# First chunk of an adaLN transformer block: row tile 1 normalised on ScalarE, scale columns in two steps, another PSUM bank order

## The chip, the cores and the metric

The kernel runs on one core of one Trainium2 chip. The metric is device time in microseconds (us), and lower is better. Engines are named as the profile names them: PE is TensorE's matmuls, PEld its weight loads, DVE is VectorE, ACT is ScalarE, POOL is GpSimd, SP is SyncE, which here issues every transfer. "q1" below is the first weight load of the q projection, and "Exp" the first Exp of the first chunk.

Ratios are the mean time of one kernel's fast runs over that of the other's in the same rounds, so they are not quite the ratio of the medians quoted.

## The reference, cut to what matters

```python
mod = (silu(c) @ w_mod)            # six rows of 1024: sa, ca, ga, sb, cb, gb
h   = layernorm(x) * (1 + ca) + sa # x is 2048 x 1024, bf16
qkv = h @ wqkv                     # 1024 -> 3 x 1024; q and k go through phi(t) = t>0 ? t+1 : exp(t)
...                                # linear attention, output projection, then x + ga * (...)
h   = layernorm(x) * (1 + cb) + sb
x   = x + gb * ((silu(h @ w_gate) * (h @ w_up)) @ w_down)   # F = 3584
```

Here ca is the scale and sa the shift of the first layernorm. The kernel computes both as columns (features on partitions) with tiny matmuls: WCA and WSA are the slices of w_mod that they need, 2 MB each, loaded in two halves.

## The kernel before

A helper records every operation, derives the semaphores, and emits one program per engine in the recorded order. The row axis is worked in four chunks of 512 rows (four row tiles of 128). Apart from the bank order, which also sets the PSUM banks of the next 40 groups of q and k matmuls, the change touches only the first chunk, in roughly the first 28 us. (A group is the eight accumulating matmuls that fill one PSUM bank.)

The loads stand in this order in SP's queue. None of them waits for any compute:

```python
for st in range(4): P.dma("x0_%d" % st, XRES[:, st, :], xv[:, st, :])   # 4 row tiles of x
ca_load(0)                 # scale columns 0-3, 1 MB
wq_load(0, 2)              # q weights, k-tiles 0 and 1
ca_load(1)                 # scale columns 4-7
wq_load(2, 2)
sa_load(1)                 # shift columns 4-7: the "first WSA half"
wq_load(4); wq_load(5); wq_load(6); wq_load(7)
sa_load(0)                 # shift columns 0-3: the "second WSA half"
# ... x of the second chunk, k weights, more x ...
```

Statistics, normalisation and transposes of the first four row tiles; `warm(n)` issues n dummy matmuls on zeros, meant to keep PE's clock up:

```python
act_stats(2)                                   # statistics of tile 2 on ACT
warm(13, bank=3)
s0_[0](); s0_[1](); s1_[0](); s0_[2](); ln1_rstd1(0); s1_[1]()   # DVE; the power -1/2 is on POOL
ln1_xn(0); tile_transposes(0); warm(2, bank=3)
s1_[2](); ln1_rstd1(1); s3_[0]()
ln1_xn(1); tile_transposes(1); warm(4, bank=3) # tile 1 normalised on DVE
# ... statistics of tiles 2 and 3 ...
ln1_xn(2); ln1_xn(3)
mod_sc(WCA, 8, range(4)); fin_ca(0, 4)         # scale columns 0-3: 32 matmuls, then one DVE op
tile_transposes(2, 3)                          # k-tile by k-tile, both tiles
h0_first(0..3, "dve")                          # k-tiles 0-3: transposed x * scale, PSUM to SBUF
raw_copy(4); raw_copy(6)                       # k-tiles 4-7 unscaled, on ACT
```

The q projection of the chunk accumulates 8 k-tiles. K-tiles 0 to 3 enter without the shift, which a bias adds later. K-tiles 4 to 7 need scale and shift, so they need the first WSA half:

```python
# k-tiles 0 and 1 of the first seven q groups (14 matmuls)
mod_sc(WCA, 8, range(4, 8)); fin_ca(4, 4)
for nt in range(7):
    if nt == 6:
        mod_sc(WSA, 0, range(4, 6))   # <- gate 1: needs the first WSA half
        fin_sa(4, 2); h0_scale(4); h0_scale(5)
    q_part(nt, qb[nt], (2, 3))
mod_sc(WSA, 0, range(6, 8)); fin_sa(6, 2); h0_scale(6); h0_scale(7)
# k-tiles 4, 5, 6 of seven groups (21 matmuls)
for nt in range(7):
    if nt == 0:
        mod_sc(WSA, 0, range(4))      # <- gate 2: needs the second WSA half
        fin_sa(0, 4, True)
    if nt == 4:
        bias_mm()                     # the shift of k-tiles 0-3, as a bias for q
    q_part(nt, qb[nt], (7,))
# eighth group, then Exp and Relu of every q group with that bias
```

Of the kernel before, what the change touches and what calls it, by code (L numbers as in the profile page):

```python
# [8 lines left out]
ACT = mybir.ActivationFunctionType  # L9
# [255 lines left out]
def bass_adaLN_cond__linear_attn_block__swiglu_ffn__prompt_kernel(  # L265
# [22 lines left out]
    with ExitStack() as es:  # L288
# [6 lines left out]
        def T(name, off, shape, dt):  # L295
            n = 1
            for s_ in shape[1:]:
                n *= s_
            assert off % 32 == 0 and off + n * mybir.dt.size(dt) <= ARENA, (name, off, shape)
            return nc.alloc_sbuf_tensor_at(name, shape, dt, offset=base + off)  # L300
# [4 lines left out]
        WCA = T("wca", 32 * KB, [128, NDT, D], BF16)  # L305
# [35 lines left out]
        HT = T("ht", 120 * KB, [128, 2, NDT, 512], BF16)  # L341
# [52 lines left out]
        P = _Prog()  # L394
# [59 lines left out]
        def warm(n=1, bank=2):  # L454
            for _ in range(n):
                P.pe("matmul", out=PS[:, bank, :], lhsT=IDENT[:], rhs=E1[:, 0, :], start=True, stop=True)
# [6 lines left out]
        def ln1_stats_ops(st):  # L463
            par, j = (st // 4) % 2, st % 4
            return [
                lambda: P.dve("bn_stats", out=STATS[:, par, j, 0, :], in_=XRES[:, st, 0:512]),
                lambda: P.dve("bn_stats", out=STATS[:, par, j, 1, :], in_=XRES[:, st, 512:1024]),
                lambda: P.dve("bn_aggr", out=MV[:, st, :], in_=STATS[:, par, j, :, :]),
            ]
# [10 lines left out]
        def ln1_xn(st):  # L480
            P.dve("tensor_scalar", out=XRES[:, st, :], in0=XRES[:, st, :],
                  scalar1=MV[:, st, 0:1], scalar2=RSTD[:, st:st + 1], op0=ALU.subtract, op1=ALU.mult)
# [7 lines left out]
        def th_dma(st):  # L490
            buf, j = (st // 4) % 2, st % 4
            xbar(HT[:, buf, :, j * 128:(j + 1) * 128], XRES[:, st, :])
# [12 lines left out]
        def mod_sc(w, c0, ms):  # L505
            for m in ms:
                for kt in range(NDT):
                    P.pe("matmul", out=PS[:, 0, c0 + m:c0 + m + 1], lhsT=w[:, kt, m * 128:(m + 1) * 128],
                         rhs=SILUC[:, kt:kt + 1], start=mod_first[0], stop=(kt == NDT - 1), skip_group_check=True)
                    mod_first[0] = False  # L510

        def fin_ca(m, n):
            P.dve("tensor_scalar", out=MODCOL[:, 0, m:m + n], in0=PS[:, 0, 8 + m:8 + m + n], scalar1=1.0, scalar2=None,
                  op0=ALU.add)

        def fin_sa(m, n, cast=False):
            if cast:
                P.dve("tensor_copy", out=MODTMP[:, m:m + n], in_=PS[:, 0, m:m + n])
            P.dve("tensor_copy", out=MODCOL[:, 1, m:m + n], in_=PS[:, 0, m:m + n])
# [12 lines left out]
        def t_view(dt, n=1):  # L532
            return PSB[:, 4 + dt // 2, (dt % 2) * 512:(dt % 2 + n) * 512]

        def h0_first(dt, eng):
            if eng == "act":
                P.act("activation", out=HT[:, 0, dt, :], in_=t_view(dt), func=ACT.Copy, scale=MODCOL[:, 0, dt:dt + 1])
            else:
                P.dve("tensor_scalar", out=HT[:, 0, dt, :], in0=t_view(dt), scalar1=MODCOL[:, 0, dt:dt + 1],
                      scalar2=None, op0=ALU.mult)  # L540

        def raw_copy(dt):
            P.act("activation", out=HT[:, 1, dt:dt + 2, :], in_=t_view(dt, 2).rearrange("p (d q) -> p d q", q=512),
                  func=ACT.Copy)

        def h0_scale(dt):
            P.dve("tensor_scalar", out=HT[:, 0, dt, :], in0=HT[:, 1, dt, :], scalar1=MODCOL[:, 0, dt:dt + 1],
                  scalar2=MODCOL[:, 1, dt:dt + 1], op0=ALU.mult, op1=ALU.add)

        def ln1_rstd1(st):  # L550
            P.dve("tensor_scalar", out=VE[:, st:st + 1], in0=MV[:, st, 1:2], scalar1=EPS, scalar2=None, op0=ALU.add)
            P.pool("tensor_tensor", out=RSTD[:, st:st + 1], in0=VE[:, st:st + 1], in1=NEGHALF[:, 0:1], op=ALU.pow)

        def ln1_xn_act(st):
            P.dve("tensor_scalar", out=NMR[:, st:st + 1], in0=MV[:, st, 0:1], scalar1=RSTD[:, st:st + 1],
                  scalar2=-1.0, op0=ALU.mult, op1=ALU.mult)
            P.act("activation", out=XRES[:, st, :], in_=XRES[:, st, :],
                  func=ACT.Identity, scale=RSTD[:, st:st + 1], bias=NMR[:, st:st + 1])
# [30 lines left out]
        s0_, s1_, s3_ = ln1_stats_ops(0), ln1_stats_ops(1), ln1_stats_ops(3)  # L589
        m2 = act_mv_ops(2)  # L590

        def tile_transposes(*js):
            for dt in range(NDT):
                for j in js:
                    c = (dt % 2) * 512 + j * 128
                    P.pe("transpose", out=PSB[:, 4 + dt // 2, c:c + 128], in_=XRES[:, j, dt * 128:(dt + 1) * 128],
                         identity=IDENT[:])
# [5 lines left out]
        s0_[2]()  # L603
        ln1_rstd1(0)
        s1_[1]()
        ln1_xn(0)
        tile_transposes(0)
        warm(2, bank=3)
        s1_[2]()
        ln1_rstd1(1)  # L610
        s3_[0]()
        ln1_xn(1)
        tile_transposes(1)
        warm(4, bank=3)
        m2[1]()
        m2[0]()
        neg_rstd(2)
# [2 lines left out]
        ln1_rstd1(3)  # L620
        ln1_xn(2)
        ln1_xn(3)
        mod_sc(WCA, 8, range(4))
        fin_ca(0, 4)
        tile_transposes(2, 3)
        warm(0, bank=3)
        h0_first(0, "dve")
        h0_first(1, "dve")
        h0_first(2, "dve")
        h0_first(3, "dve")  # L630
        raw_copy(4)
        raw_copy(6)
        P.act("activation", out=ACTWARM[:], in_=SILUC[:], func=ACT.Exp)

        phi_ctr = [0]
# [32 lines left out]
        def q_part(nt, bank, dts):  # L668
            for dt in dts:
                P.pe("matmul", out=PS[:, bank, :], lhsT=WQK[:, dt, nt * 128:(nt + 1) * 128],  # L670
                     rhs=HT[:, 0, dt, :], start=(dt == 0), stop=(dt == 7))
# [3 lines left out]
        def next_bank():  # L675
            i = qk_ctr[0]
            qk_ctr[0] += 1
            return (i + 1) % 8 if i < 40 else i % 5 + 1

        def q_group(ch, nt):  # L680
            buf, bank = ch % 2, next_bank()
# [45 lines left out]
            P.dma("mdr%d" % i, dst[:], MDR[i].unsqueeze(0).to_broadcast([128, D]))  # L727

        def q_phase_chunk0(side):
            qb = [1, 2, 3, 4, 6, 5, 7]  # L730
            for nts, dts in ((range(6), (0,)), (range(2), (1,)), ((6,), (0, 1)), (range(2, 6), (1,))):
                for nt in nts:
                    q_part(nt, qb[nt], dts)
            mod_sc(WCA, 8, range(4, 8))
            fin_ca(4, 4)
            for nt in range(7):
                if nt == 6:
                    mod_sc(WSA, 0, range(4, 6))
                    fin_sa(4, 2)
                    for dt in (4, 5):  # L740
                        h0_scale(dt)
                q_part(nt, qb[nt], (2, 3))
            mod_sc(WSA, 0, range(6, 8))
            fin_sa(6, 2)
            for dt in (6, 7):
                h0_scale(dt)
            act_stats(4)
            for dt in (4, 5, 6):
                for nt in range(7):
                    q_part(nt, qb[nt], (dt,))  # L750
            for nt in range(7):
                if nt == 0:
                    mod_sc(WSA, 0, range(4))
                    fin_sa(0, 4, True)
                    for f in ln_ops[1]:
                        f()
                    ln1_rstd1(5)
                if nt == 4:
                    bias_mm()
                q_part(nt, qb[nt], (7,))  # L760
            for f in act_mv_ops(4):
                f()
            neg_rstd(4)
            ln1_xn(5)
            ln1_xn(4)
            th_dma(5)
            th_dma(4)
            q_phi = lambda nt: phi_evac(qb[nt] if nt < 7 else 0, PQT[:, nt, 0:512], bias=BIASQ[:, nt:nt + 1])
            for i, dt in enumerate(range(NDT)):
                P.pe("matmul", out=PS[:, 0, :], lhsT=WQK[:, dt, 896:1024], rhs=HT[:, 0, dt, :], start=(i == 0),  # L770
                     stop=(i == 7))
            for dt in range(4):
                h0_shift(dt)
            for nt in range(8):
                q_phi(nt)
                for f in side.get(nt, []):
                    f()
            qk_ctr[0] = 0
# [93 lines left out]

        P.dma("wo", WO[:], wov)
        G_BANKS = [0] + [next_bank() for _ in range(4)]

        MB = next_bank()
# [197 lines left out]
        for ch in range(NCH):  # L1074
            nxt = ch + 1 if ch + 1 < NCH else None
            for ft in range(NFT):
                q = 14 * ch + ft // 2
# [13 lines left out]
                if ch == 0 and ft % 2 == 0 and ft < 14:  # L1091
                    i = ft // 2
# [11 lines left out]
            for j in range(4):  # L1104
# [8 lines left out]
                for nh in range(2):  # L1113
                    i = nh
# [52 lines left out]
```

## Time and profile before

| | before |
|---|---|
| first measurement | 835.99 us, 835.11 to 836.0, 3 runs |
| span of the profiled run | 832.9 us, granted clock 1.0 |

From the page of the kernel before: the busy line, and the chain that ended last, by engine.

```profile
PE 821.7 (99%) x4053; PEld 379.3 (46%) x4132; DVE 301.0 (36%) x657; ACT 195.8 (24%) x335; POOL 43.2 (5%) x56
...
PE 96%; DMA 1%; DVE 1%; SPq 1%; issue 1%; ACT 0%; DVEq 0%
```

Nearly all of the change lies in the first 3% of the span. The chain of the same kernel in order of time, cut to the lines around the first WSA half (columns: start, length, what), says something else about that stage:

```profile
7.95 11.88 DMA wsa<-in_w_mod_dram
19.82 0.05 issue
19.87 3.23 PE ps L178 x42
...
```

From 7.95 to 19.82 us the end of the program hangs on the transfer of the first WSA half, not on a compute engine (before that, on SP issuing loads). The stretch table of the kernel before (columns: stretch, length, busy us of PE, PEld, DVE, ACT, POOL, granted clock, DMA share, GB/s) shows: the 16 DMA engines are full (a share of about 1).

```profile
13.00:20.00 7.00, 6.46 (x61) 3.20 (x64) 1.18 (x4) 3.15 (x4) 0.00 (x0) 1.00 1.08 368
20.00:26.00 6.00, 5.95 (x64) 3.20 (x64) 1.76 (x6) 0.00 (x0) 0.00 (x0) 1.00 1.08 360
...
29.00:45.00 16.00, 15.95 (x75) 7.24 (x74) 15.20 (x49) 15.33 (x28) 1.68 (x3) 1.00 1.03 253
```

The timeline of weight loads before (columns: start, length, engine, operation, shapes, count; in brackets the idle time before it and what ended it) shows the places. They are q1 at 12.96, gate 1 at 19.86 after 0.78 us of waiting, and gate 2 at 25.59 us:

```profile
12.96 0.56 PEld L178 LDWEIGHTS ps<-ht,wqk 128*128 128x128 bf16 x4 [0.22 <-issue]
13.80 0.10 PEld L178 LDWEIGHTS ps<-ht,wqk 128*128 128x128 bf16 x1 [0.28 <-ACT ht L178]
14.07 0.33 PEld L178 LDWEIGHTS ps<-ht,wqk 128*128 128x128 bf16 x3 [0.18 <-DVE ht L178]
14.71 0.98 PEld L178 LDWEIGHTS ps<-ht,wqk 128*128 128x128 bf16 x6 [0.31 <-ACT ht L178]
...
16.81 2.28 PEld L178 LDWEIGHTS ps<-ht,wqk 128*128 128x128 bf16 x12
19.86 0.47 PEld L178 LDWEIGHTS ps<-siluc,wsa 128*128 128x128 bf16 x16 [0.78 <-DMA wsa<-in_w_mod_dram]
...
25.59 1.01 PEld L178 LDWEIGHTS ps<-siluc,wsa 128*128 128x128 bf16 x32 [0.17 <-DMA wsa<-in_w_mod_dram]
```

Weight loads run ahead of the matmuls that use them, so their waits are longer than PE's. At gate 1 PE's matmuls themselves stood idle 0.29 us, by their modelled ends:

```profile
19.87 0.55 PE L178 MATMUL ps<-siluc,wsa 128*128 128x1 bf16 x16 [0.29 <-DMA wsa<-in_w_mod_dram]
```

And the first Exp of ACT in the timeline before, the end of the stage:

```profile
28.86 0.69 ACT L178 ACTIVATE e<-ps,biasq 128x512 bf16<-128x512 f32 x1 [0.29 <-DVE mv L178]
```

### The profile page before, as it was taken

Reading aid. Unit: us, or ns where it says so; the run is one execution under the profiler, and the core shown is the slowest. Engines: PE = TensorE matmul, PEld = TensorE weight load, DVE = VectorE, ACT = ScalarE, POOL = GpSimd, SP = SyncE. Lnnn points to the kernel's source line nnn. Section 1 sums busy time; section 2 is a strip of 40 time slices with the busy share of each in tenths; the row PEclk is TensorE's granted clock in tenths of the full one; section 3 lists DMA queues with packets and bytes.
Section 4 is the critical chain, followed back from the end, with each engine's and each line's share of the span. In section 5 each row is a group of like instructions: output and inputs, shape, how many; then the busy total and the mean of one; then the engine's idle time right before and its main releaser. Section 6 shows DMA issues by size and latency. Waiting matters only on the chain.

```text
span 832.9 us, 10029 instructions
## 1 busy us (share of the span) xinstructions
PE 821.7 (99%) x4053; PEld 379.3 (46%) x4132; DVE 301.0 (36%) x657; ACT 195.8 (24%) x335; POOL 43.2 (5%) x56
## 2 busy tenths in 40 slices
PE   7999999999999999999999999999999999999998
PEld 4544444444444444444444444444444444444444
DVE  5797985657873212110222111122111212111111
ACT  3667642222332111110111111111111111111011
POOL 1000000000050000030000003000000300000000
DMA  9969734938197895610455571045557104553000
GB/s 311 300 151 227 208 70 146 200 103 303 35 223 241 257 268 152 179 50 13 114 152 152 151 189 39 13 114 153 153 152 194 32 13 121 153 150 94 1 26 25
DMA packets 190940, 117.17 MB, mean 141 GB/s; under 512 B 49576, under 2 KB 174640, under 8 KB 190896
## 3 DMA queue, kind: packets, MB, share of 16 engines
q1 hardware_dynamic: 190896, 116.55, 50.7%
q8 instruction: 32, 0.52, 0.3%
q14 instruction: 12, 0.10, 0.0%
HBM read 100.67 MB, written 4.33 MB: 126 GB/s over the span
## 4 chain that ended last, share of the span: by engine, by line
PE 96%; DMA 1%; DVE 1%; SPq 1%; issue 1%; ACT 0%; DVEq 0%
PE ps L178 96%; DMA wsa<-in_w_mod_dram 1%; SPq L178 1%; DVE acc L178 0%; DVE xres L178 0%; DVE mhl L178 0%; ACT mw L178 0%; DVE ve L178 0%; DVE ut L178 0%; DVE mean L178 0%; DVE msq L178 0%; DVE sumx L178 0%; DVEq L249 0%
## 5 line engine op out<-in xcount | busy, mean ns | idle before, releaser
L178 PE MATMUL ps<-h2t,guu 128*128 128x512 bf16 x878 | 210.2, 379 | 0.9
L178 PE MATMUL ps<-h2t,gug 128*128 128x512 bf16 x878 | 210.0, 380 | 0.9
L178 DVE TENSOR_TENSOR at<-sg,ps 128x512 bf16<-128x512 bf16 x112 | 77.1, 688 | 296.1 <-PE ps L178 285.0
L178 ACT ACTIVATE sg<-ps 128x512 bf16<-128x512 f32 x112 | 66.9, 597 | 310.3 <-PE ps L178 298.9
L178 PEld LDWEIGHTS ps<-h2t,guu 128*128 128x128 bf16 x896 | 87.6, 98 | 105.8
L178 PEld LDWEIGHTS ps<-h2t,gug 128*128 128x128 bf16 x896 | 87.4, 98 | 105.4
L178 PE MATMUL ps<-wd_a,at 128*128 128x512 bf16 (+2 forms) x519 | 112.9, 373 | 0.5
L178 PE MATMUL ps<-ht,wqk 128*128 128x512 bf16 x499 | 110.7, 380 | 0.9 <-DVE ht L178 0.3
L178 PE MATMUL ps<-wd_b,at 128*128 128x512 bf16 (+2 forms) x388 | 85.5, 373 | 0.5
L178 PEld LDWEIGHTS ps<-wd_a,at 128*128 128x128 bf16 x528 | 51.0, 98 | 59.8
L178 PEld LDWEIGHTS ps<-ht,wqk 128*128 128x128 bf16 x512 | 49.2, 98 | 59.2 <-ACT ht L178 0.6
L178 DVE TENSOR_TENSOR ut<-att,gb_b 128x512 bf16<-128x512 bf16 (+1 forms) x32 | 13.7, 427 | 167.6 <-ACT att L178 167.6
L178 ACT ACTIVATE att<-ps 128x512 bf16<-128x512 f32 (+1 forms) x32 | 17.4, 591 | 182.1 <-PE ps L178 182.1
L178 PEld LDWEIGHTS ps<-wd_b,at 128*128 128x128 bf16 x396 | 38.2, 98 | 44.7
L178 PE MATMUL ps<-pk,xres 128*128 128x512 bf16 x250 | 56.4, 380 | 0.3
L178 PE MATMUL ps<-mw,pqt 128*128 128x512 bf16 x250 | 55.8, 380 | 0.4
L178 POOL TENSOR_SCALAR h2t<-h2t,modcol 128x512 bf16<-128x512 bf16 x32 | 28.5, 905 | 395.5 <-DMA h2t<-xn 379.2
L178 ACT ACTIVATE e<-ps 128x512 bf16<-128x512 f32 x56 | 33.0, 602 | 32.8 <-PE ps L178 24.7
L178 PEld LDWEIGHTS ps<-mw,pqt 128*128 128x128 bf16 x256 | 24.9, 98 | 29.7 <-DVE xres L178 0.2
L178 PEld LDWEIGHTS ps<-pk,xres 128*128 128x128 bf16 x256 | 24.7, 98 | 29.8 <-issue 0.4
L178 ACT ACTIVATE junk<-xres 128x1024 bf16<-128x1024 bf16 x24 | 25.4, 1058 | 36.0 <-DVE xres L178 35.8
L178 POOL TENSOR_TENSOR rstd<-ve,neghalf 128x1 f32<-128x1 f32 (+2 forms) x17 | 14.0, 838 | 215.7 <-DVE ve L178 176.8
(98 smaller groups left out, 341.4 us busy)
## 6 DMA issues: line engine op xcount, KB each, us to landing
gug<-in_B_w_gate_dram SPq DMA_DIRECT2D x56, 512.0 KB, 4.0
guu<-in_B_w_up_dram SPq DMA_DIRECT2D x56, 512.0 KB, 5.3
xres<-in_A_x_dram SPq DMA_DIRECT2D x20, 256.0 KB, 7.8
rb<-recip_den SPq DMA_DIRECT2D x8, 512.0 KB, 12.0
stgx<-in_w_mod_dram SPq DMA_DIRECT2D x2, 2048.0 KB, 8.6
wd_a<-in_B_w_down_dram SPq DMA_DIRECT2D x4, 1024.0 KB, 7.4
out_dram<-xres SPq DMA_DIRECT2D x31, 128.0 KB, 1.7
xres<-in_A_x_dram SPq DMA_DIRECT2D x3, 1024.0 KB, 14.2
```

What stands on the lines that cost most here:

```text
L178: return getattr(e, method)(**kw)
```

## The change

The intent is to bring the q projection's first matmul forward. Row tile 1 moves to ACT, so that DVE is free sooner for tiles 2 and 3. Only the scale columns that are needed first are made first. One of the two raw copies moves to DVE. The bank order follows the order in which the transpose banks come free. (The joint transposes of tiles 2 and 3, k-tile by k-tile, are in both versions.)

```diff
-        def raw_copy(dt):
-            P.act("activation", out=HT[:, 1, dt:dt + 2, :], in_=t_view(dt, 2).rearrange(...), func=ACT.Copy)
+        def raw_copy(dt, eng):
+            dst, src = HT[:, 1, dt:dt + 2, :], t_view(dt, 2).rearrange("p (d q) -> p d q", q=512)
+            if eng == "act": P.act("activation", out=dst, in_=src, func=ACT.Copy)   # lines joined here
+            else:            P.dve("tensor_copy", out=dst, in_=src)
@@ statistics and normalisation
+        s1_[2]()
+        ln1_rstd1(1)
         ln1_xn(0)
         tile_transposes(0)
-        warm(2, bank=3)
-        s1_[2]()
-        ln1_rstd1(1)
+        warm(5, bank=3)
         s3_[0]()
-        ln1_xn(1)
+        ln1_xn_act(1)          # one DVE op for the bias, then one 1024-column pass on ACT
         tile_transposes(1)
-        warm(4, bank=3)
+        warm(1, bank=3)
@@ scale columns and copies
-        mod_sc(WCA, 8, range(4))
-        fin_ca(0, 4)
+        mod_sc(WCA, 8, range(2))
+        fin_ca(0, 2)
         tile_transposes(2, 3)
-        warm(0, bank=3)
         h0_first(0, "dve")
         h0_first(1, "dve")
-        h0_first(2, "dve")
-        h0_first(3, "dve")
-        raw_copy(4)
-        raw_copy(6)
+        raw_copy(4, "dve")
+        raw_copy(6, "act")
@@ next_bank
-            return (i + 1) % 8 if i < 40 else i % 5 + 1
+            return (1, 2, 3, 4, 6, 7, 5, 0)[i % 8] if i < 40 else i % 5 + 1
@@ q_phase_chunk0
-            qb = [1, 2, 3, 4, 6, 5, 7]
-            for nts, dts in ((range(6), (0,)), (range(2), (1,)), ((6,), (0, 1)), (range(2, 6), (1,))):
+            qb = [1, 2, 3, 4, 6, 7, 5]
+            for nt in range(4):
+                q_part(nt, qb[nt], (0,))
+            mod_sc(WCA, 8, range(2, 4))
+            fin_ca(2, 2)
+            for dt in (2, 3):
+                h0_first(dt, "dve")
+            for nts, dts in (((4, 5), (0,)), (range(6), (1,)), ((6,), (0, 1))):
```

More of the change, by code (lines that the diff above doesn't have):

```diff
@@ L540, in h0_first @@
                       scalar2=None, op0=ALU.mult)
-        def raw_copy(dt):
-            P.act("activation", out=HT[:, 1, dt:dt + 2, :], in_=t_view(dt, 2).rearrange("p (d q) -> p d q", q=512),
-                  func=ACT.Copy)
+        def raw_copy(dt, eng):
+            dst, src = HT[:, 1, dt:dt + 2, :], t_view(dt, 2).rearrange("p (d q) -> p d q", q=512)
+            if eng == "act":
+                P.act("activation", out=dst, in_=src, func=ACT.Copy)
+            else:
+                P.dve("tensor_copy", out=dst, in_=src)
         def h0_scale(dt):
```

## The prediction

> What bounds the kernel. The page shows PE busy 99% of 832.9 us, and the chain that ended last is 96% PE. The change touches only the first 28 us. There the chain in order of time is not PE: until 7.95 us it is SP issuing loads, then 11.88 us of waiting for the first half of WSA (shift columns, landing at 19.83 us), then PE, without a gap over 0.1 us. The stretch table shows the DMA engines full (share 1.06 to 1.09, 350 to 380 GB/s) from 7 to 28 us. The waits show a second gate: PE's weight loads idle 0.17 us for the other WSA half, landing at 25.59 us. From there to 45 us PE is busy 19.3 of 19.4 us. So before 19.83 us PE has slack: its weight loads sat 0.78 us, its matmuls 0.29 us idle there.
>
> What the change does, costed from the trace:
> - Row tile 1's normalisation leaves DVE (0.55 us) for ScalarE: one 1024-column pass (1.06 us for such a pass) plus a 0.15 us DVE op for the bias. ScalarE is free only at 8.27 us, so the pass ends near 9.5 us, where DVE's ended at 9.05. Its transposes come 0.4 us later, in time that dummy matmuls filled before.
> - DVE's chain for tiles 2 and 3 starts earlier: I put the last normalisation's end at 11.2 us instead of 11.85, so the first q matmul comes at 12.6 instead of 13.2 us.
> - Half of the first scale-column matmuls (16 of 32, about 0.4 us) move between the q matmuls. That is later PE work, and eats most of those 0.6 us.
> - One raw copy goes from ScalarE (1.02 us) to DVE: estimated 0.8 us, from 0.48 us for 512 columns there; the Trainium skill ("VectorE: DVE Perf Modes", the perf-mode tier table) caps copies out of PSUM at the 2x mode, and the 0.48 us fits that. It removes PE's waits for ScalarE (0.3 us twice) at 13.8 and 14.7 us.
> - The bank order makes later groups use banks as they come free. PE waited for no bank between 28 and 45 us, so nothing is gained.
> The joint transposes of tiles 2 and 3 are already k-tile by k-tile before.
>
> Net: PE reaches the first WSA wait 0.2 to 0.7 us earlier, all off the critical path: WSA's issue does not depend on compute (SP's queue waits for no compute before 29 us), its landing does not move, and everything behind it is the same work. PE waits longer at 19.8 us, and the gain is given back there in full. The Trainium skill ("Trainium Kernel Development and Optimization", Key Constraints) says that all queues share the 16 DMA engines; the full share in the trace agrees, so no reordering of compute speeds this transfer.
>
> Prediction: 835.8 us, the old time within its spread (835.11 to 836.0), range 834.3 to 837.0. Faster by over 2%: 0.005; within: 0.99; slower: 0.005.
>
> In the profile: first q matmul near 12.6 us; PE's idle for WSA grown from 0.78 to 1.0 us or more on weight loads; WSA still landing near 19.8 and 25.6 us; PE's matmuls after the bias columns starting near 28.4 us as before.
>
> What would make it wrong: PE reaching the first WSA gate over 0.8 us later than before (DVE's two late scalings holding up bank 5 or k-tile 2); WSA landing some tenths elsewhere by itself; too few dummy matmuls, so that PE's clock falls back (matmul starts 0.43 us apart instead of 0.22, as before 6 us); a bank conflict in later chunks.

## The result, and the profile after

| | before | changed |
|---|---|---|
| median | 835.72 us | 835.36 us |
| range | 835.11 to 836.0, 4 runs | 834.85 to 836.0, 4 runs |
| ratio, 95% interval | | 0.9997, 0.998 to 1.0014 |
| span of the profiled run | 832.9 | 833.0 |

The time is the same. From the page of the changed kernel (its DVE share of 3% stands for most of its length at 84 to 97 and 211 to 217 us; the column "span - Exp" below shows that it cost nothing measurable):

```profile
PE 821.9 (99%) x4053; PEld 379.9 (46%) x4132; DVE 301.7 (36%) x659; ACT 196.2 (24%) x335; POOL 43.6 (5%) x56
...
PE 94%; DVE 3%; DMA 1%; SPq 1%; issue 1%; ACT 0%; DVEq 0%; ACTq 0%
```

Its chain in order of time hangs on the same transfer, and the stretch table shows the same full DMA engines:

```profile
8.79 11.24 DMA wsa<-in_w_mod_dram
20.04 0.05 issue
20.08 0.57 PE ps L178 x16
...
```

```profile
13.00:20.00 7.00, 6.56 (x72) 3.44 (x71) 1.71 (x5) 2.14 (x3) 0.00 (x0) 1.00 1.07 366
20.00:26.00 6.00, 5.86 (x56) 3.11 (x58) 1.75 (x6) 0.00 (x0) 0.00 (x0) 1.00 1.09 361
...
29.00:45.00 16.00, 15.89 (x74) 7.31 (x75) 15.16 (x50) 15.29 (x28) 1.88 (x3) 1.00 1.06 263
```

The timeline of weight loads after, and its first Exp:

```profile
12.64 0.56 PEld L178 LDWEIGHTS ps<-ht,wqk 128*128 128x128 bf16 x4 [0.22 <-issue]
13.31 0.66 PEld L178 LDWEIGHTS ps<-siluc,wca 128*128 128x128 bf16 x16
13.91 1.85 PEld L178 LDWEIGHTS ps<-ht,wqk 128*128 128x128 bf16 x10
...
16.87 2.28 PEld L178 LDWEIGHTS ps<-ht,wqk 128*128 128x128 bf16 x12
20.08 0.47 PEld L178 LDWEIGHTS ps<-siluc,wsa 128*128 128x128 bf16 x16 [0.94 <-DMA wsa<-in_w_mod_dram]
...
25.79 1.02 PEld L178 LDWEIGHTS ps<-siluc,wsa 128*128 128x128 bf16 x32 [0.17 <-DMA wsa<-in_w_mod_dram]
```

```profile
29.05 0.69 ACT L178 ACTIVATE e<-ps,biasq 128x512 bf16<-128x512 f32 x1 [0.25 <-PE ps L178]
```

The changed kernel issues its first q weight load 0.32 us earlier (12.64 against 12.96). It reaches the last block before gate 1 no earlier at all (16.87 against 16.81), because 16 scale-column loads now stand in the middle (the line at 13.31). Then it waits until WSA has landed, 0.2 us later in this execution. From there the two run alike: the Exp comes 8.97 us after gate 1 in the changed kernel and 9.00 before, and the span ends 803.95 and 804.04 us after the Exp.

One execution of each is thin evidence, because the transfers move by some tenths between executions. In this pair ACT could start on row tile 2 (its data landed) at 6.28 us after and at 5.95 before. So the experiments below are read through the same marks, each within its own execution.

### The profile page after: what moved, and what is told of

It reads as the page before. It is cut to its first block, busy times and chain, and to the rows that moved or that the text cites. A ratio compares the mean times of both kernels' runs of the same rounds, so it can differ in the third digit from the quotient of the medians.

```text
span 833.0 us, 10031 instructions
## 1 busy us (share of the span) xinstructions
PE 821.9 (99%) x4053; PEld 379.9 (46%) x4132; DVE 301.7 (36%) x659; ACT 196.2 (24%) x335; POOL 43.6 (5%) x56
## 4 chain that ended last, share of the span: by engine, by line
PE 94%; DVE 3%; DMA 1%; SPq 1%; issue 1%; ACT 0%; DVEq 0%; ACTq 0%
PE ps L178 94%; DMA wsa<-in_w_mod_dram 1%; DVE acc L178 1%; SPq L178 1%; DVE xres L178 0%; DVE pkt L178 0%; DVE mhl L178 0%; DVE ht L178 0%; DVE e L178 0%; DVE pqt L178 0%; ACT e L178 0%; ACT mw L178 0%; DVE ve L178 0%; DVE modcol L178 0%; DVE ut L178 0%
## 5 line engine op out<-in xcount | busy, mean ns | idle before, releaser
L178 PEld LDWEIGHTS ps<-pk,xres 128*128 128x128 bf16 x256 | 24.8, 98 | 29.8 <-issue 0.4
L178 POOL TENSOR_TENSOR rstd<-ve,neghalf 128x1 f32<-128x1 f32 (+2 forms) x17 | 14.2, 850 | 215.7 <-DVE ve L178 176.4
```

Source lines behind the costliest of these rows:

```text
L178: return getattr(e, method)(**kw)
```

## The experiments

The theory: in the first chunk the landing of the first WSA half sets the pace, and the time is that landing plus a constant, whatever PE does before it, as long as PE is there first. The rival: the stage is PE work, and a gain of a few tenths went through but is hidden in the noise, or was never made. Twelve kernels were run.

This table collects the marks from the profile of each run, in us. "Wait" is the idle time of weight loads at gate 1, "gate 1" the first WSA weight load. "Exp - gate 1" and "span - Exp" are differences of the other columns (the span is known to 0.1 us). A dash marks runs where PE waited for nothing at gate 1.

| kernel | q1 | last block | wait | gate 1 | Exp | Exp - gate 1 | span | span - Exp |
|---|---|---|---|---|---|---|---|---|
| before | 12.96 | 16.81 | 0.78 | 19.86 | 28.86 | 9.00 | 832.9 | 804.04 |
| changed | 12.64 | 16.87 | 0.94 | 20.08 | 29.05 | 8.97 | 833.0 | 803.95 |
| e0 changed again | 12.32 | 16.55 | 0.44 | 19.27 | 28.22 | 8.95 | 832.2 | 803.98 |
| e1 8 matmuls less before gate 1 | 12.49 | 16.72 | 1.40 | 18.67 | 27.92 | 9.25 | 831.9 | 803.98 |
| e2 8 matmuls less, late | 12.26 | 16.48 | 1.00 | 19.77 | 28.81 | 9.04 | 831.1 | 802.29 |
| e3 WSA later | 12.88 | 17.11 | 3.41 | 22.80 | 33.43 | 10.63 | 837.5 | 804.07 |
| e4 tile 1 alone | 12.34 | 16.19 | 1.36 | 19.83 | 28.81 | 8.98 | 832.8 | 803.99 |
| e5 without tile 1 | 12.87 | 17.10 | 1.45 | 20.82 | 29.81 | 8.99 | 833.8 | 803.99 |
| e6 waits filled | 12.75 | 16.98 | - | 19.80 | 29.38 | 9.58 | 833.3 | 803.92 |
| e7 later loads held back | 12.38 | 16.61 | 0.88 | 19.77 | 28.74 | 8.97 | 832.8 | 804.06 |
| e8 WSA later, wait filled | 12.41 | 16.64 | 1.13 | 22.64 | 31.59 | 8.95 | 835.6 | 804.01 |
| e9 half WSA, before | 13.57 | 17.43 | - | 19.82 | 28.93 | 9.11 | 833.0 | 804.07 |
| e10 half WSA, changed | 12.68 | 16.91 | - | 19.30 | 28.41 | 9.11 | 832.5 | 804.09 |
| e11 half WSA, tile 1 alone | 12.50 | 16.35 | - | 18.75 | 27.86 | 9.11 | 831.9 | 804.04 |

Two columns are nearly constant. In seven runs (before, changed, e0, e2, e4, e5 and e7) the Exp comes 8.95 to 9.04 us after gate 1, although PE's weight loads had waited there for 0.44 to 1.45 us. In all runs but e2, where matmuls were left out late, the span ends 803.92 to 804.09 us after the Exp. So in the gated runs with an undisturbed clock the span is about landing + 9.0 + 804.0, and the span of one execution differs from another's by what the landing differs: e0 and e5 issue their loads in the same order, have gate 1 at 19.27 and 20.82 us, and spans of 832.2 and 833.8. The second column also covers the bank order: the span ends 803.99 to 804.07 us after the Exp with the old one (before, e4, e9, e11) and 803.92 to 804.09 with the new one, so it gained and cost nothing that shows.

The waits in the table are those of weight loads. PE's matmuls waited about 0.5 us less at gate 1: 0.29 us before, 0.44 in the changed kernel, 0.96 in e5, and in e0 no wait of theirs is listed at all. So in an execution in which WSA lands as early as in e0, the gate barely holds PE, and a gain in front of it may come through in part.

The second WSA half is nearly as late as the first. From gate 2 (the first weight load of the second half) to the Exp all fourteen profiles need 3.19 to 3.29 us. In the seven runs weight loads wait 0.16 to 0.23 us at gate 2, which PE's matmuls hardly feel; had the first half alone come earlier, the second would soon have set the pace. e1 shows this.

### e0: the changed kernel again

No edit.

> The changed kernel once more, as yardstick for this call. Theory (the transfers of the shift columns gate the first chunk): same as before within 0.1%, about 835.4 us; PE's weight loads idle 0.5 to 1.2 us at the first gate near 20 us; the two landings of WSA within 0.4 us of 19.8 and 25.6. Rival (PE-bound there, gain lost in noise): ratio to before 0.9995 or less with an interval that excludes 1.

Measured: 835.64 us (5 runs; before 835.42, 11 runs), ratio 0.9999, interval 0.9987 to 1.0012. Gates 1 and 2 opened at 19.27 and 24.97 us, 0.5 and 0.6 us before the times expected and 0.1 and 0.2 us outside the theory's window, and PE's wait was a little below its range (0.44). A ratio that excludes 1 did not appear. The miss of the window says that the landing moves more between executions than expected.

### e1 and e2: the same eight matmuls taken away before the gate, and late

Both give a wrong result.

```diff
 # e1                                          (k-tiles 2, 3 of four q groups, in front of gate 1)
-                q_part(nt, qb[nt], (2, 3))
+                if nt >= 4:
+                    q_part(nt, qb[nt], (2, 3))
 # e2, in k_group                              (k-tiles 2, 3 of four k groups of the last chunk)
+                if ch == 3 and nt < 4 and dt in (2, 3):
+                    continue
```

> The changed kernel with 8 q matmuls (k-tiles 2 and 3 of four q groups, 8 x 0.216 = 1.7 us of PE) left out in front of the first WSA gate; wrong result on purpose. Theory: PE's idle at the gate near 20 us grows by about 1.7 us (weight loads from 0.94 to about 2.6), the first Exp of the first chunk still starts near 29.0 us, and the time stays within 0.4 us of the changed kernel. Rival (first chunk is PE-bound): 1.7 us less, about 833.7 us.

> The changed kernel with the same number of matmuls (8, k-tiles 2 and 3 of four k groups) left out in the last chunk of the first projection, where no transfer gates PE; wrong result on purpose. Both theories: about 1.7 us less than the changed kernel, 833.7 us, if PE sets the pace there. It is the control that shows that a loss of 8 matmuls can be seen at all. Its first 28 us repeat those of the changed kernel.

Measured: e2 took 833.38 us (6 runs, 833.15 to 833.57), ratio to before 0.9973, interval 0.9961 to 0.9985. In its profile the span ends 802.29 us after the Exp instead of 804.0, which is 1.7 us for 8 matmuls of 0.216 us. (By the medians e2 is 2.3 us below the changed kernel; the rest is within the 1.6 us over which that kernel's runs spread.) So a loss of eight matmuls is seen where PE sets the pace.

e1 took 836.75 us (6 runs, 834.34 to 838.23), ratio 1.0012, interval 0.9997 to 1.0027. The rival's 833.7 us did not appear: eight matmuls less before the gate did not make the kernel faster. In the profiled run PE's wait was 1.40 us. That is the changed kernel's 0.94, plus the 1.72 us of matmuls left out, less the 1.41 us by which WSA landed earlier in this execution, plus the 0.15 us by which the last block came earlier: in this execution the work taken away turned into waiting in full. With the first half so early, the second half held PE longer (0.51 us against 0.17), and the Exp came 9.25 us after gate 1 instead of 8.97:

```profile
18.67 0.47 PEld L178 LDWEIGHTS ps<-siluc,wsa 128*128 128x128 bf16 x16 [1.40 <-DMA wsa<-in_w_mod_dram]
...
24.73 0.86 PEld L178 LDWEIGHTS ps<-siluc,wsa 128*128 128x128 bf16 x32 [0.51 <-DMA wsa<-in_w_mod_dram]
```

But the theory's number was missed too. It expected the changed kernel's time within 0.4 us, and five of the six runs were at 836.17 to 838.23 us. The per-run clock points to the reason: those five have a mean granted clock of 0.998 or 0.996, and the sixth, which was the profiled one, has 1.0 and 834.34 us. A mean clock lower by 0.002 over 833 us is 1.7 us. Those five runs have no trace, so where their clock fell is not seen. With 1.7 us taken off per 0.002 of clock, the six runs would lie at 834.3 to 835.3 us, with a median of 834.9 against 835.64 for the changed kernel in these rounds. By this rough estimate up to some 0.7 us of the 1.7 may have come through and been lost again to the clock; that nothing at all comes through is not shown. In the same rounds, 2 of 11 runs of the kernel before have 0.998, and they took 837.47 and 837.74 us; its other 9 took 834.56 to 836.32. e3 has a lower clock too, with a trace.

### e3: the first WSA half issued 1 MB later

```diff
-        sa_load(1)
         wq_load(4)
         ...
         wq_load(7)
+        sa_load(1)
```

> The changed kernel with the first WSA half (1 MB) issued after the four single wq loads (another 1 MB) instead of before them. Theory: it lands 2 to 3 us later (near 22.5 us), PE's idle at the gate grows by as much, the first Exp starts 2 to 2.7 us later and the time is 837.4 to 838.2 us. Rival (the transfer has slack and PE's own work sets the first chunk): the time stays within 0.5 us of the changed kernel.

Measured: 839.81 us (6 runs, 837.61 to 840.38), ratio 1.0047, interval 1.0033 to 1.006. The rival (no change) is refuted: moving one transfer behind 1 MB of others, with not an instruction of PE changed, costs about 4 us. The landing moved by 2.7 us (gate 1 at 22.80 against 20.08). But the time moved by more than the 2 to 2.7 us that the theory allowed. The rest is in the timeline of weight loads of e3, after the wait:

```profile
22.80 0.47 PEld L178 LDWEIGHTS ps<-siluc,wsa 128*128 128x128 bf16 x16 [3.41 <-DMA wsa<-in_w_mod_dram]
...
24.12 0.56 PEld L178 LDWEIGHTS ps<-ht,wqk 128*128 128x128 bf16 x4
24.83 0.15 PEld L178 LDWEIGHTS ps<-ht,wqk 128*128 128x128 bf16 x1 [0.15 <-issue]
25.25 0.15 PEld L178 LDWEIGHTS ps<-ht,wqk 128*128 128x128 bf16 x1 [0.28 <-issue]
25.68 0.15 PEld L178 LDWEIGHTS ps<-ht,wqk 128*128 128x128 bf16 x1 [0.28 <-issue]
...
28.21 1.83 PEld L178 LDWEIGHTS ps<-ht,wqk 128*128 128x128 bf16 x9 [0.24 <-issue]
```

and in its stretch table, 24.8 to 28.2 us, where the granted clock is 0.51:

```profile
24.80:28.20 3.40, 3.18 (x8) 1.21 (x8) 0.42 (x2) 1.71 (x3) 0.00 (x0) 0.51 1.09 358
```

From 24.8 to 28.2 us the weight loads start 0.43 us apart instead of 0.216, with no wait for another engine or a transfer listed. Eight matmuls at half speed cost 8 x 0.215 = 1.7 us, which is what Exp - gate 1 grew by (10.63 against 8.97). The Trainium skill ("TensorE: Matmul & The Clock Gate", Part 1: The HAM clock gate) gives 426.7 and 215.7 ns as the start-to-start of 512-column matmuls with the cold and the warm clock, and a window of about 3.4 us by which the clock is judged; both spacings and the length of the slow stretch agree with this trace. So a wait at the gate has a second price, once it is long enough: the clock drops after it. In e3, five of six runs have 0.998 or 0.996; the one with 1.0 took 837.61 us, which is what the theory had expected of all.

### e8: e3 with its wait filled

```diff
                 if nt == 6:
+                    for _ in range(12):       # adds zero: E1 still holds zeros here
+                        P.pe("matmul", out=PS[:, qb[5], :], lhsT=IDENT[:], rhs=E1[:, 0, :],
+                             start=False, stop=False)
                     mod_sc(WSA, 0, range(4, 6))
```

> The late-WSA kernel (839.8 us) with 12 matmuls that add zero to a q bank (12 x 0.216 = 2.6 us) put into PE's 3.4 us wait for the late transfer; the result is unchanged. Theory: of that kernel's 4.4 us loss 2.7 us are the later landing and 1.7 us are PE's clock, which fell to half from 24.8 to 28.2 us after the long wait. With the wait filled the clock stays at 1.0, the first Exp again starts 9.0 us after the landing instead of 10.6, and the time falls to about 838.0 us although PE has more to do. Rival (the whole loss is the transfer): no better than 839.8 us.

Measured: 838.23 us (6 runs, 837.57 to 838.73), ratio 1.0035, interval 1.0022 to 1.0048, and a clock of 1.0 in all six. From e8's stretch table and its timeline:

```profile
26.00:29.00 3.00, 3.00 (x33) 1.59 (x32) 0.00 (x0) 2.30 (x4) 0.00 (x0) 1.00 1.09 360
```

```profile
22.64 0.46 PEld L178 LDWEIGHTS ps<-siluc,wsa 128*128 128x128 bf16 x16 [1.13 <-DMA wsa<-in_w_mod_dram]
```

Twelve more matmuls made the kernel faster: 838.23 against 839.81 us. The two ran in different rounds, in which the kernel before had medians of 834.88 and 835.42; by the ratios (1.0035 against 1.0047) the gain is 1.0 us, and their intervals overlap, so the times alone would not settle it. The clock (1.0 in six of six runs against one of six) and the profiles do. In the profiles it is 1.68 us (Exp - gate 1 fell from 10.63 to 8.95). This separates the two parts of the loss in e3's profile: some 2.6 us of later landing, which stays (gate 1 at 22.64 against 20.08), and 1.7 us of clock, which goes. The rival that the whole loss is the transfer is refuted by the profiles.

### e4 and e5: the change in two parts

e4 is the kernel before with only the second block of the diff (tile 1 on ACT, dummies moved). e5 is the changed kernel with that block put back.

```diff
 # e4, against before                      # e5, against the changed kernel: the reverse
+        s1_[2]()
+        ln1_rstd1(1)
         ln1_xn(0)
         ...
-        ln1_xn(1)
+        ln1_xn_act(1)
```

> The kernel before, with row tile 1 on ScalarE and the moved dummies as the only part of the change. Theory: the chain for tiles 2 and 3 gives 0.3 to 0.6 us (first q weight load near 12.3 to 12.7 us against 12.96), PE reaches the gate that much earlier and waits that much longer; the first Exp starts 9.0 us after the first WSA half is there, and the span is that start plus 804.0 us, as in the four profiles so far. Time 835.0 to 836.0 us. Rival (the earlier tiles carry through): 0.3 us or more less at an equal landing, so the first Exp 8.7 us or less after the landing.

> The changed kernel with row tile 1 put back on VectorE: two-step scale columns, the raw copy on VectorE and the bank order stay. Theory: first q weight load near 13.0 us as before; the 16 moved scale-column matmuls (0.43 us) cost PE what the two waits for ScalarE (0.3 us each before) give back, so PE reaches the gate within 0.3 us of the kernel before; first Exp again 9.0 us after the landing, time 835.0 to 836.0 us.

Measured: e4 835.39 us (4 runs, 835.05 to 836.04), ratio 1.0003, interval 0.9988 to 1.0018; e5 835.73 us (4 runs, 834.89 to 836.3), ratio 1.0004, interval 0.999 to 1.0017. The kernel before in those rounds: 835.28.

The profile of e4 is the clearest exhibit, since its transfers came as in the profile of before (row tile 2 ready at 5.96 against 5.95 us, gate 1 at 19.83 against 19.86). Its timeline of weight loads:

```profile
12.34 0.56 PEld L178 LDWEIGHTS ps<-ht,wqk 128*128 128x128 bf16 x4 [0.22 <-issue]
...
16.19 2.28 PEld L178 LDWEIGHTS ps<-ht,wqk 128*128 128x128 bf16 x12
19.83 0.47 PEld L178 LDWEIGHTS ps<-siluc,wsa 128*128 128x128 bf16 x16 [1.36 <-DMA wsa<-in_w_mod_dram]
```

q1 is 0.62 us earlier than before, the last block is 0.62 us earlier, the wait at gate 1 is 0.58 us longer, and the Exp is 0.05 us earlier. Row tile 1 on ACT does what it was meant to do, and the gate takes it back whole. The theory holds; the rival's 8.7 us did not appear (8.98).

e5 has q1 at 12.87, near 13.0 as expected, and its last block at 17.10. That is 0.29 us after before's, at the edge of what was expected, with the reason given there wrong. From q1 to the last block e4 and before need 3.85 us, e5 and the changed kernel 4.23, and so does every other kernel with the split columns. The 0.38 us go with the 16 scale-column matmuls that were moved in (0.43 us); this is by count, since no run has the split columns alone. Nothing was given back for the waits for ACT that the split version does not have.

### e6: work put into the waits

```diff
-                if nt == 6:
-                    mod_sc(WSA, 0, range(4, 6)); fin_sa(4, 2); h0_scale(4); h0_scale(5)   # lines joined
                 q_part(nt, qb[nt], (2, 3))
+            mod_sc(WSA, 0, range(4, 6)); fin_sa(4, 2); h0_scale(4); h0_scale(5)           # lines joined
...
-                if nt == 0:     # second WSA half, and statistics of row tile 5
+                if nt == 2:
...
-                if nt == 4:     # bias
+                if nt == 6:
```

> The changed kernel with work put into the two waits: the seventh q group's two matmuls (0.43 us) go in front of the first gate, the second WSA half is used two q groups later, the bias one later. Theory: PE's wait at the first gate shrinks by 0.43 us and the second gate's wait (0.17 us) goes; part of it comes back as a wait for the first scaled k-tile, so the first Exp starts 8.6 to 8.9 us after the landing instead of 9.0, the gain is 0.1 to 0.4 us and below what the times resolve: 835.0 to 835.7 us. Rival (all is PE work, there is no wait to fill): 9.0 us after the landing.

Measured: 835.81 us (5 runs, 835.71 to 837.53), ratio 1.001, interval 0.9997 to 1.0022. This missed: the waits for WSA are gone in its profile, but the Exp comes at 29.38 us, 9.58 us after gate 1. (Some 0.2 us of the growth is the mark: without a wait, the weight loads at 19.80 run ahead of their matmuls at 20.02.) Two other waits matter now in the timeline of weight loads of e6, both for DVE:

```profile
20.81 0.47 PEld L178 LDWEIGHTS ps<-siluc,wsa 128*128 128x128 bf16 x16 [0.34 <-DVE modcol L178]
...
29.34 4.65 PEld L178 LDWEIGHTS ps<-ht,wqk 128*128 128x128 bf16 x23 [0.48 <-DVE mv L178]
```

The changed kernel's weight loads have these waits too (0.29 and 0.27 us), but there its matmuls go on; here the matmuls stand idle as well, for 0.25 and 0.18 us. The bias stands two q matmuls (0.43 us) later in PE's order, but not later after gate 1, because the seventh group's two matmuls went in front of it. Of the edits it was not tried which costs what. One of the five runs had a clock of 0.998 (837.53 us); it has no trace. Filling a wait with the work that used to hide a later latency is no gain.

### e7: the later loads held back

```diff
-        sa_load(1)
+        sa1 = sa_load(1)
         ...
         sa_load(0)
+        P.wait_for("sp", [sa1])     # x of the second chunk and the k weights come after it
```

> The changed kernel with the SP queue holding back the later loads (x of the second chunk, the k weights) until the first WSA half has landed, so that they do not share the DMA engines with it. Theory (the transfers set the time): both WSA halves land earlier, by 0.5 to 1.5 us, PE's waits go, and the time falls by 0.3 to 1.0 us (834.4 to 835.1). If the engines serve the loads strictly in order of issue, the landings stay and so does the time. Rival (PE-bound): earlier landings change nothing.

Measured: 835.09 us (5 runs, 834.93 to 836.08), ratio 0.9999, interval 0.9986 to 1.0011; gate 1 at 19.77, gate 2 at 25.47. The hold worked: x of the second chunk was issued from 19.74 us on instead of about 14.4. The time forecast reached up to 835.1, so the time alone decides nothing, and neither does one landing, since landings move by more than 1 us between executions. The stretch table of e7 says more: without the later loads the engines were as full as before (369 against 368 GB/s).

```profile
13.00:20.00 7.00, 6.62 (x82) 3.57 (x80) 1.46 (x5) 1.89 (x3) 0.00 (x0) 1.00 1.08 369
```

So the loads that are issued later took nothing that this run could show from the earlier ones. The Trainium skill ("DMA: Bandwidth & Descriptors", Queues, rings and completion order) says that each of the 16 engines consumes the descriptors of a ring in order; this run is in line with that, and so is e3, where 1 MB put in front moved the landing by 2.7 us. At the 365 GB/s of the stretch tables 1 MB takes 2.9 us. As far as these runs show, what lands when is therefore set mainly by the bytes in front in the queue.

### e9, e10, e11: the gates lifted

All three load only half of each WSA piece and use it twice (a wrong result), so that both halves land before PE asks for them. e9 is based on the kernel before, e10 on the changed one, e11 on e4.

```diff
-            P.dma("wsa%d" % p, WSA[:, :, 512 * p:512 * p + 512], wmv[:, :, 512 * p:512 * p + 512])
+            P.dma("wsa%d" % p, WSA[:, 0:4, 512 * p:512 * p + 512], wmv[:, 0:4, 512 * p:512 * p + 512])
...
-                    ... lhsT=w[:, kt, m * 128:(m + 1) * 128], ...
+                    ... lhsT=w[:, kt % 4 if w is WSA else kt, m * 128:(m + 1) * 128], ...
```

> The kernel before with only half of each WSA piece loaded (k-tiles 0 to 3, used twice; wrong result on purpose), so that the first half lands about 1.4 us and the second 2.8 us earlier, and neither gates PE. Theory: no PE wait for WSA; the first gate is passed near 19.3 us, the first Exp at about 28.3 us, span about 832.3 us.

> The same edit on the changed kernel. Theory: with the gates lifted, what the change gained in front of them comes through: first q weight load 12.3 to 12.7 us, the first Exp 0.1 to 0.4 us earlier than in the half-WSA kernel before (its lead at the first q matmul less the 0.38 us that the split scale columns take). Rival (the change gains nothing in front of the gates either): within 0.1 us or later.

> The same edit on the kernel with row tile 1 on ScalarE alone. Theory: it comes out first of the three, about 0.38 us ahead of the half-WSA changed kernel and 0.5 to 0.7 us ahead of the half-WSA kernel before at the first Exp (near 27.7 us), because the split scale columns, the raw copy on VectorE and the bank order only add 0.4 us of PE work between the first q matmul and the gate. Rival (the three parts belong together): the changed kernel is as early or earlier.

Measured (4 runs each; before in the same rounds 834.88):

| | median | range | Exp | wait at the gates |
|---|---|---|---|---|
| e9, before | 834.57 us | 834.54 to 835.21 | 28.93 | none |
| e10, changed | 834.65 us | 834.45 to 835.0 | 28.41 | none |
| e11, tile 1 alone | 834.34 us | 834.14 to 834.82 | 27.86 | none |

With the gates lifted, Exp - gate 1 is 9.11 us in all three. So PE's own arrival at the gate now sets the end, and the order of the three is the expected one in the profiles. The last block and gate 1 of e11, without a wait:

```profile
16.35 2.28 PEld L178 LDWEIGHTS ps<-ht,wqk 128*128 128x128 bf16 x12
18.75 0.66 PEld L178 LDWEIGHTS ps<-siluc,wsa 128*128 128x128 bf16 x16
```

e11 is ahead of e10 by 0.55 us in the profile and by 0.3 us in the medians; 0.38 us of it is the split columns (q1 to last block 3.85 against 4.23). For e10 against e9 the evidence is weaker. In e9's profiled execution the first scale columns landed late (PE waited 0.96 us for WCA, and row tile 2 was ready only at 7.21 us), so its Exp at 28.93, against an expected 28.3, is no fair measure, and the medians of e9 and e10 differ by 0.08 us the wrong way. What the whole change is worth without the gate stays open, somewhere between nothing and the few tenths that the profiles show. That tile 1 alone is worth at least as much is what the medians say too, though their ranges overlap.

Apart from e2, which leaves out work where PE sets the pace, no version tried beats both kernels by anything that the times resolve.

## Why the prediction was right

- 835.8 us was forecast (834.3 to 837.0), 835.36 measured, the same as before. By itself this proves little: the 0.6 us that the rival theory could have let through are 0.07% of the time, and the forecast would have held then too. What supports the mechanism is the marks within each profile, and e1 to e4.
- **The main step held.** "WSA's issue does not depend on compute (...), its landing does not move, and everything behind it is the same work." In seven runs the Exp comes 8.95 to 9.04 us after gate 1, however early PE was there. Taking 1.7 us of PE work away in front of the gate did not make the kernel faster (e1), the same work taken away later gave 1.7 us (e2), and a later landing made the span longer by that much (e8: 2.56 and 2.6 us) or by more (e3). That the gain is given back "in full" in every execution is not shown: in e0 the gate barely held PE's matmuls. Of the page that the prediction cites for this, the trace shows the full engines; that several queues share them no run shows, since SP alone issues transfers.
- **"The first q matmul comes at 12.6 instead of 13.2 us" was half a reading error.** The matmul timeline lacks a record there (13 of 14 in the profile before), so 13.2 was the second matmul; the weight loads give 12.96. At equal transfers the gain is nevertheless the predicted 0.6 us: 12.34 against 12.96 in e4. In the nine profiles that share the changed kernel's PE program up to there (changed, e0, e1, e2, e3, e6, e7, e8, e10), q1 lies between 12.26 and 12.88.
- **"One 1024-column pass (1.06 us for such a pass)" was too short.** With per-row scale and bias the pass took 1.24 us. That fell into time that dummies filled, and cost nothing.
- **"It removes PE's waits for ScalarE (0.3 us twice)" was wrong.** Those were waits of weight loads, not of matmuls. Before, 14 q matmuls and 32 small ones take 3.85 us from q1 to the last block; 14 x 0.216 + 32 x 0.027 (16 small ones take 0.43 us) is 3.88. So there was no gap for PE. The copy itself took DVE 0.68 us, where 0.8 was estimated. The Trainium skill ("Perfetto Trace Analysis", Per-engine timelines, the part on the tensor engine) notes that PE's queue can pull weight loads ahead of matmuls in flight; a weight load may wait, then, while the array is busy, and that agrees with this sum.
- **"PE reaches the first WSA wait 0.2 to 0.7 us earlier" came out as -0.06 us in the pair of profiles**, and between 0.30 us later (e3) and 0.33 us earlier (e2) in the eight other profiles with the same PE program up to there (0.26, 0.33 and 0.20 in e0, e2 and e7, whose code is the changed kernel's up to the gate), all against the one profile of before. An earlier arrival of the whole change is therefore not shown. The split of the scale columns was sized about right (0.4 us forecast, 0.38 between the marks). The term that was mis-sized is what the waits for ScalarE would give back: 0.3 us twice by the forecast, nothing by the count. In the pair q1 was also only 0.32 us earlier, with row tile 2 ready 0.33 us later. The predicted wait of 1.0 us or more at the gate was accordingly 0.94 us, and 0.44 to 1.00 in e0, e2 and e7.
- **"WSA still landing near 19.8 and 25.6 us"** held on average only. In eight profiles with the same order of loads up to it and full WSA pieces (before, changed, e0, e1, e2, e4, e5, e7) gate 1 opened between 18.67 and 20.82 us. This spread of 2.15 us is larger than anything that the change did, and through it the spans differ from run to run.
- **A risk was placed in the wrong spot.** The prediction feared a falling clock from too few dummies. A lower clock does occur, in 3 of 31 runs of the kernel before (all at 0.998, 837.47 to 837.96 us, against 834.52 to 836.32 us for the others) and in none of the nine runs of the changed kernel; nine are too few to tell. It occurs in one of five runs of e6 too. Where it fell in those four was not traced. A long wait at the gate brings it on: in e3 it is seen soon after the wait, and with the wait filled it is gone (e8). With 1.7 us of work less in front of the gate it struck in five runs of six (e1), which fits, but was not traced.

## What to carry to other kernels

Before you speed up the work in front of a transfer, find out whether the transfer or the work arrives last. A chain of waits in order of time, cut to the stage that the change touches, showed it here, where the shares of the whole span said "PE 96%". Time gained in front of such a gate becomes waiting, and a wait of some three microseconds can also drop PE's clock, so that arriving earlier can end later unless dummy matmuls fill it. When a change has several parts, count the matmuls between two marks for each part: one part here won 0.6 us, another lost 0.4 of it, and the time could show neither.

## What the Trainium skill lacked or had wrong

- "TensorE: Matmul & The Clock Gate", Part 1: its table has the clock fall after at least one idle window of about 3.4 us. Here a wait of 2.92 us between matmuls, by their modelled ends (3.41 us between weight loads, which equals the table's window), was enough, and the slow stretch began only 2.0 us after PE was at work again (e3: gate 1 at 22.80, slow from 24.8 to 28.2 us).
- "DMA: Bandwidth & Descriptors": nothing on how far the landing of the same load moves between executions of the same queue. Here a 1 MB piece behind some 4 MB of others opened its gate between 18.67 and 20.82 us.
